# Turning round the second matrix product of a fused attention and MLP kernel: the activations stationary, the weights moving

## The chip, the cores and the metric

The kernel runs on one core of a Trainium2 chip. The metric is the device time of one execution in microseconds (us). The engines are named as the profile names them: PE is TensorE (the matmuls), PEld its loads of the stationary operand, DVE is VectorE, ACT is ScalarE, POOL is GpSimd and SP is SyncE, which issues the DMAs here.

## The reference

An attention with two branches, over q, k and v of 8 batches, 8 heads, 576 positions and 64 channels, feeds a two-layer MLP over 4608 tokens of 512 channels:

```python
q_d = q.reshape(B, H, Sd, factor, D).mean(axis=3)      # factor 4, so do k_d, v_d
out_up = np.repeat(sm_attn(q_d, k_d, v_d), factor, axis=2)
mask = np.abs(pos[:, None] - pos[None, :]) < factor    # a band of 7 keys
scores = np.where(mask, scale * np.matmul(q, k.transpose(0, 1, 3, 2)), -1e9)
attn_out = out_up + softmax(scores) @ v
x = attn_out.transpose(0, 2, 1, 3).reshape(B * S, H * D)
h = x @ w_in                                           # 512 x 2048
g = np.maximum(0.01 * h, h)
return g @ w_out                                       # 2048 x 512
```

## The kernel before

**Precision.** Both products of the MLP are made from operands that are split in a high and a low part in the fp32r format (xh and xl, wih and wil, gh and gl, woh and wol). Each product of two tiles is then three matmuls: high x high, high x low and low x high.

**Tiling.** The 4608 tokens are cut in twelve chunks: chunk 0 of 512 tokens (worked in two halves of 256, `TOP`), chunk 1 of 256 and ten chunks of 384. The 2048 hidden channels are cut in 16 blocks f of 128. `STEPS` lists (chunk, first and last token, f): 48 steps of 256 tokens and 160 of 384. In chunk 0 the first half runs eight blocks ahead of the second, so the first half is through with f = 15 while the second is at f = 7 (`LEAD` is 8).

**The first product** is `up_proj` (matmuls on line 811). For each step it takes a PSUM bank `hp` (two of them) and writes 128 hidden channels x n tokens in it, with w_in stationary and x moving: 4 blocks of input channels x 3 = 12 matmuls. `leaky` follows: two activations on ACT (lines 822 and 823) write gh and the full-precision value back to the bank, and one subtraction on DVE (line 825) writes gl and gives the bank back. gh and gl have three buffers each.

**The second product** is `down_proj` (matmuls on line 847). For each step it takes gh and gl, and for each of four blocks e of 128 output channels makes three matmuls with a 128 x 128 piece of w_out stationary and the n tokens moving. Output channel block e gathers in bank `acc{e}`, over all 16 steps of the chunk: four banks, one buffer each, used again by the next chunk. In chunk 0 both halves of 256 tokens share a bank, so all four are evacuated at the chunk's end. With two banks `hp`, two banks `pt` for the attention and four accumulators, all eight banks of PSUM are in use.

**The output.** `store` copies a bank to SBUF (line 876 on ACT; line 873 on DVE for every second block of the first and the last chunk) and issues one DMA. The buffer is `o`, with two buffers of 384 tokens. Chunk 0's four copies of 512 tokens go to an old token buffer, `x0`, which `outbuf` holds until they have been sent. The output in memory is channels x tokens, and the host transposes it.

**The order of the work.** Every part is a Python generator, and `Order.run` lists the instructions of each engine in an order that it works out from estimated durations (`COST` for ACT, DVE and POOL; for PE the number given at the place; for DMAs a formula in `run`), from ranks, and from when buffers come free. `up_proj` has rank 4999 and `down_proj` 5000, behind all the attention's work. The engines then run these fixed lists, each waiting for its semaphores. A change in one estimate can therefore move instructions anywhere.

**The rest.** Batch 0's attention is made with matmuls, for the other seven the band's products are made on POOL (lines 669 and 730) and summed on DVE (675 and 736). The weights are loaded, converted and split in the first 115 us (lines 287 to 308). `landing` puts finished tokens in x (lines 767 to 782); x has two buffers, `x0` and `x1`.

Of the kernel before, what the change touches and what calls it, by code (L numbers as in the profile page):

```python
# [21 lines left out]
BLK, NBLK = 9, 64  # L22
# [12 lines left out]
LEAD = 8  # L35
HEADS = 2
FREE = 9
LSPLIT = 14
HALFS = 4
HF1 = 21  # L40
# [155 lines left out]
def attn_moe(ctx: ExitStack, tc, qkt, vd, qb, kb, vb, vwb, band, identb, w_in, w_out, ident, edge, out):  # L196
# [4 lines left out]
    ps = ctx.enter_context(tc.tile_pool(name="ps", bufs=1, space=PSUM))  # L201

    bufs = dict(head=HEADS, qk=1, vs=1, qk_d=2, qblk=1, v_d=2, su_vd=2, su_half=1, st_d=2, pd=1, ptd=2, outd=2, q=2, k=2, v=2, s=3, st_l=3, prod=2, up=1,
                xloc=2, lst=3, gh=3, gl=3, o=2, hp=2, pt=2, x0=1, x1=1, stage=3, stage2=4, acc0=1, acc1=1, acc2=1, acc3=1,
                su_vw=NC, su_vs=NC, su_pt=2)
    od = Order(bufs)

    def slot(*tags):
        return (yield ("slot", tags, 0))
# [5 lines left out]
    def bank(s):  # L215
        return ps.tile([128, 512], F32, name=s.tag, tag=s.tag, bufs=bufs[s.tag])
# [572 lines left out]
    def up_proj():  # L789
        i = 0  # L790
        while i < len(STEPS):
            ch, a, z, f = STEPS[i]
            n = z - a
            per = 0.012 + n / 2400
            m = 2 if (ch, a, f) == (0, 0, 0) else 1
            if f == 0:
                tx = 0.0 if m > 1 else (yield from wait(("x", ch, a), LANDED[ch, a]))
            hps = []
            for k in range(m):
                tw = yield from wait(("w", f + k, 0))  # L800
                s_h = yield from slot("hp")
                hps.append((s_h, bank(s_h), weight(f + k, 0), tw))
            xh, xl = (x[:, :, a:z] for x in xt[ch])
            for c in range(NC):
                if m > 1:
                    tx = yield from wait(("x", 0, 0, c))
                ws = slice(c * 128, (c + 1) * 128)
                for k, (s_h, hp, w, tw) in enumerate(hps):
                    t = yield from op("PE", 3 * per, tx, tw, s_h.t)
                    for j, (h, x) in enumerate(((1, xh), (1, xl), (0, xh))):  # L810
                        nc.tensor.matmul(hp[:, :n], w[h][:, ws], x[:, c], start=c + j == 0, stop=c == NC - 1 and j == 2)  # L811
                    if c == NC - 1:
                        od.spawn(-10, leaky(i + k, n, s_h, hp, t))
            if f == NF - 1:
                od.signal(("done", ch), t)
            i += m
# [12 lines left out]

    def down_proj():  # L830
        for i, (ch, a, z, f) in enumerate(STEPS):
            n = z - a
            last = z == CHUNKS[ch][1]
            per = 0.012 + n / 2400
            tg = yield from wait(("g", i))
            tw = yield from wait(("w", f, 1))
            s_g, s_l, gh, gl = gs.pop(i)
            w = weight(f, 1)
            for e in range(NE):
                if (a, f) == (0, 0):  # L840
                    s_a = yield from slot(f"acc{e}")
                    accs[ch, e] = s_a, bank(s_a)
                s_a, acc = accs[ch, e]
                es = slice(e * 128, (e + 1) * 128)
                t = yield from op("PE", 3 * per, tg, tw, s_a.t)
                for j, (h, g) in enumerate(((1, gh), (1, gl), (0, gh))):
                    nc.tensor.matmul(acc[:, a:z], w[h][:, es], g[:, :n], start=(a, f, j) == (0, 0, 0),  # L847
                                     stop=f == NF - 1 and j == 2, skip_group_check=ch == 0)
                if f == NF - 1 and last:
                    od.spawn(-5, store(ch, e, s_a, acc, t))  # L850
            s_g.free(t)
            s_l.free(t)

    first = []

    def outbuf():
        yield from wait(("xbuf", 0))
        s_x = yield from slot("x0")
        first.append(sb(s_x, [128, NE, 512], F32))
        od.signal("first", s_x.t)  # L860
        s_x.free((yield from wait("sent", NE)))

    def store(ch, e, s_a, acc, t):
        base, n = CHUNKS[ch][:2]
        if ch == 0:
            s_o, to = None, (yield from wait("first"))
            o = first[0][:, e]
        else:
            s_o = yield from slot("o")
            o, to = sb(s_o, [128, OMAX], F32)[:, :n], s_o.t  # L870
        if ch in (0, len(CHUNKS) - 1) and e % 2:
            t = yield from op("DVE", n, t, to)
            nc.vector.tensor_copy(out=o, in_=acc[:, :n])  # L873
        else:
            t = yield from op("ACT", n, t, to)
            nc.scalar.copy(out=o, in_=acc[:, :n])
        s_a.free(t)
        t = yield from load(out[e * 128:(e + 1) * 128, base:base + n], o, 512 * n, t)
        if s_o:
            s_o.free(t)  # L880
        else:
            od.signal("sent", t)

    su = tc.tile_pool(name="su", bufs=1)
    sup = su.__enter__()
# [15 lines left out]
    with tc.manual_schedule():  # L901
# [19 lines left out]
        od.spawn(0, edges())  # L921
        od.spawn(0, opened())
        od.spawn(30, over())
        od.spawn(-1, outbuf())
        od.spawn(5000, down_proj())
        od.spawn(4999, up_proj())
        for b in range(BANDED, B):
# [10 lines left out]
    attn_moe.order = od  # L938


_OUTS = [((DM, B * S), 'float32')]
# [58 lines left out]
```

## Time and profile before

| | |
|---|---|
| median of 3 runs | 939.52 us (938.36 to 941.15) |
| the profiled execution | 939.17 us, of which the span from first to last instruction 937.4 us |
| granted TensorE clock, mean | 0.991 |
| PE busy | 911.9 us, 97% |
| DVE, ACT, POOL busy | 598.3, 428.8, 610.4 us |
| data read and written in HBM | 104.47 and 9.44 MB |

The profile shows one execution. A group's row gives the line in the kernel, the engine, the operation, the tiles written and read, the number of instructions, then the busy time and the mean duration in ns, then the idle time of the engine ahead of them and what ended it. Matmuls overlap, so the duration of one is no measure of its price: the distance between starts is. In the list of waits each row has the waiting instruction, what it waited for, the sum in us, the number of times and the longest. In the chain that ended last a row has its start in us, its length and the number of instructions merged in it. In the timeline a row has start and duration in us, and in brackets the idle time ahead of it.

### The profile page before, as it was taken

The numbers are of one execution on the slowest core, as the hardware profiler recorded it, in microseconds if no ns is written. First come the engines' busy times: TensorE is split into PE (matmuls) and PEld (weight loads), VectorE is DVE, ScalarE is ACT, GpSimd is POOL, SyncE is SP. The second block draws the span as 40 slices with busy tenths as digits, with TensorE's granted clock in tenths as the row PEclk, the third lists the DMA queues.
The fourth block names the chain that finished last, engine by engine and source line by source line (L and its number), as shares of the span: only waits on it lengthen the run. The fifth ranks groups of instructions, "written<-read, shape, count | busy, mean of one in ns | idle before, by whom it ended". The sixth has DMA issues, their size and how long they took to land.

```text
span 937.4 us, 16213 instructions
## 1 busy us (share of the span) xinstructions
PE 911.9 (97%) x6114; PEld 892.3 (95%) x6114; DVE 598.3 (64%) x934; ACT 428.8 (46%) x1178; POOL 610.4 (65%) x349
## 2 busy tenths in 40 slices
PE   6898999999999999999999999999999999999997
PEld 4698999998999999999999999999999999999997
DVE  5999998898978876864655873862754744211111
ACT  4876755655546444654324553523423424312221
POOL 4677899999989978963975963983984972000000
PEclk7999999999999999999999999999999999999999
DMA  9886656656554652541432541530431410000000
GB/s 255 265 280 204 197 171 184 183 159 204 150 154 151 205 155 78 184 148 57 138 91 55 182 154 32 152 113 27 131 103 36 141 51 12 34 1 1 35 1 35
DMA packets 58783, 114.97 MB, mean 123 GB/s; under 512 B 6976, under 2 KB 23616, under 8 KB 58704
## 3 DMA queue, kind: packets, MB, share of 16 engines
q1 hardware_dynamic: 58704, 113.93, 40.1%
q8 instruction: 48, 0.79, 0.4%
q14 instruction: 31, 0.25, 0.1%
HBM read 104.47 MB, written 9.44 MB: 122 GB/s over the span
## 4 chain that ended last, share of the span: by engine, by line
PE 89%; DVE 2%; ACT 0%; issue 0%; DMA 0%; DVEq 0%; ACTq 0%
PE hp L811 41%; PE acc L847 41%; PE pt L418 2%; PE pt L455 2%; PE pt L479 2%; PE pt L767 1%; DVE gl L825 0%; DMA out_dram<-o 0%; DVE stage L295 0%; DVE v_d L369 0%; DVE x L295 0%; DVE s L675 0%; DVE x L873 0%; ACT pd L434 0%; DVE qblk L385 0%
## 5 line engine op out<-in xcount | busy, mean ns | idle before, releaser
L811 PE MATMUL hp<-x,wih 128*128 128x384 f32 (+1 forms) x1664 | 406.7, 329 | 7.2 <-DVE gl L825 7.2
L669 POOL TENSOR_TENSOR prod<-q,k 128x1344 f32<-128x1344 f32 x84 | 260.6, 3103 | 84.1 <-DVE xloc L736 68.1
L811 PEld LDWEIGHTS hp<-x,wih 128*128 128x128 f32 x1664 | 287.2, 189 | 10.0 <-DVE gl L825 8.3
L730 POOL TENSOR_TENSOR prod<-v,s 128x1344 f32<-128x1344 f32 x84 | 262.3, 3126 | 20.0 <-DVE xloc L736 19.7
L847 PE MATMUL acc<-gh,woh 128*128 128x384 f32 (+1 forms) x832 | 272.4, 327 | 0.0
L811 PE MATMUL hp<-x,wil 128*128 128x384 f32 (+1 forms) x832 | 269.7, 324 | 0.2 <-POOL wil L308 0.2
L847 PE MATMUL acc<-gh,wol 128*128 128x384 f32 (+1 forms) x832 | 268.8, 323 | 0.0
L847 PE MATMUL acc<-gl,woh 128*128 128x384 f32 (+1 forms) x832 | 268.8, 323 | 0.0
L825 DVE TENSOR_TENSOR gl<-hp,gh 128x384 fp32r<-128x384 f32 (+1 forms) x208 | 108.5, 523 | 248.8 <-ACT hp L823 247.4
L822 ACT ACTIVATE gh<-hp 128x384 fp32r<-128x384 f32 (+1 forms) x208 | 97.4, 468 | 296.3 <-PE acc L847 289.1
L811 PEld LDWEIGHTS hp<-x,wil 128*128 128x128 f32 x832 | 157.1, 189 | 0.6 <-POOL wil L308 0.6
L847 PEld LDWEIGHTS acc<-gh,woh 128*128 128x128 f32 x832 | 156.5, 188 | 0.7 <-issue 0.4
L847 PEld LDWEIGHTS acc<-gl,woh 128*128 128x128 f32 x832 | 156.5, 188 | 0.0
L847 PEld LDWEIGHTS acc<-gh,wol 128*128 128x128 f32 x832 | 156.4, 188 | 0.0
L675 DVE TENSOR_REDUCE s<-prod 128x21 f32<-128x1344 f32 x84 | 129.3, 1539 | 7.0 <-POOL prod L669 6.9
L736 DVE TENSOR_REDUCE xloc<-prod 128x192 f32<-128x1344 f32 x84 | 129.5, 1541 | 5.9 <-POOL prod L730 5.8
L823 ACT ACTIVATE hp<-hp 128x384 f32<-128x384 f32 (+1 forms) x208 | 96.5, 464 | 0.0
L434 ACT ACTIVATE pd<-pt,st_d 128x144 f32<-128x144 f32 x84 | 32.0, 381 | 47.5 <-DVE st_d L431 36.3
L754 ACT COPY up<-outd 128x576 f32<-128x576 f32 x84 | 52.2, 675 | 0.1
L774 DVE TENSOR_TENSOR pt<-pt,up 128x384 f32<-128x384 f32 x42 | 37.8, 899 | 22.3 <-PE pt L767 18.5
L457 ACT COPY ptd<-pt 72x288 f32<-72x288 f32 x64 | 25.0, 397 | 31.6 <-PE pt L455 31.3
L369 DVE TENSOR_REDUCE v_d<-vs 72x128 f32<-72x512 f32 x56 | 37.5, 669 | 1.3 <-DMA vs<-in_vd_dram 1.2
(111 smaller groups left out, 709.4 us busy)
## 6 DMA issues: line engine op xcount, KB each, us to landing
k<-in_kb_dram SPq DMA_DIRECT2D x84, 288.0 KB
v<-in_vb_dram SPq DMA_DIRECT2D x84, 288.0 KB
qk<-in_qkt_dram SPq DMA_DIRECT2D x32, 576.0 KB
vs<-in_vd_dram SPq DMA_DIRECT2D x56, 144.0 KB
q<-in_qb_dram SPq DMA_DIRECT2D x84, 96.0 KB
out_dram<-o SPq DMA_DIRECT2D x40, 192.0 KB
x<-in_w_in_dram SPq DMA_DIRECT2D x10, 511.8 KB
x<-in_w_out_dram SPq DMA_DIRECT2D x7, 511.8 KB
```

Source lines behind the costliest of these rows:

```text
L369: nc.vector.tensor_reduce(out=v_d[:, p0:p1], in_=vs, axis=AX.X, op=ALU.add)
L669: nc.gpsimd.tensor_tensor(out=prv, in0=q[:, a - j0:z - j0].unsqueeze(2).to_broadcast([128, n, W, D]), in1=view(k, (a - j0) * D, [[D, n], [ ...
L675: nc.vector.tensor_reduce(out=s[:, p, a - j0:z - j0], in_=prv, axis=AX.X, op=ALU.add)
L730: nc.gpsimd.tensor_tensor(out=prv, in0=view(v, 0, [[1, nj], [nv, D], [1, W]]), in1=s[:, p, :nj].unsqueeze(2).to_broadcast([128, nj, D, W]) ...
L736: nc.vector.tensor_reduce(out=xl_t[:, :nj, p], in_=prv, axis=AX.X, op=ALU.add)
L754: nc.scalar.copy(out=up[:, pp], in_=outd[b][:, 2 * u + pp].unsqueeze(2).to_broadcast([128, SD, FAC]))
L774: nc.vector.tensor_tensor(out=xv, in0=xv, in1=upv, op=ALU.add)
L811: nc.tensor.matmul(hp[:, :n], w[h][:, ws], x[:, c], start=c + j == 0, stop=c == NC - 1 and j == 2)
L822: nc.scalar.activation(out=gh[:, :n], in_=hp[:, :n], func=AF.Prelu, alpha=0.01)
L823: nc.scalar.activation(out=hp[:, :n], in_=hp[:, :n], func=AF.Prelu, alpha=0.01)
L825: nc.vector.tensor_tensor(out=gl[:, :n], in0=hp[:, :n], in1=gh[:, :n].bitcast(F32), op=ALU.subtract)
L847: nc.tensor.matmul(acc[:, a:z], w[h][:, es], g[:, :n], start=(a, f, j) == (0, 0, 0), stop=f == NF - 1 and j == 2, skip_group_check=ch == 0)
```

## The change

The second product is turned round. A 128-token slice of g is now the stationary operand, and 512 columns of w_out (all output channels) move. A bank holds 128 tokens x 512 channels instead of 128 channels x n tokens. Each step makes 3 matmuls for each tile of 128 tokens (9 for 384 tokens, 6 for 256) where it made 12. The three products are now in the order gh x woh, gh x wol, gl x woh.

A chunk of 384 tokens needs three banks, and takes any of `acc0` to `acc2`, whichever comes free first; chunk 0 takes all four, two for each half. From chunk 1 on the first product may take `acc3` as a bank beside the two `hp`.

The output is stored as tokens x channels. Each bank is copied in two halves of 256 channels, with one DMA each, through `o`, which now has three buffers of 256 columns in the place of two of 384. Both copies are on ACT; in the last chunk the second is on DVE. `outbuf` is gone, so the token buffer `x0` isn't held for chunk 0's output. The planner's estimate for one matmul of 512 columns is 0.226 us.

```diff
+ACC = tuple(f"acc{e}" for e in range(4))
...
-                xloc=2, lst=3, gh=3, gl=3, o=2, hp=2, ...
+                xloc=2, lst=3, gh=3, gl=3, o=3, hp=2, ...
...
-                s_h = yield from slot("hp")
+                s_h = yield from slot("hp", *(ACC[3:] if ch else ()))
...
     def down_proj():
         for i, (ch, a, z, f) in enumerate(STEPS):
...
-            for e in range(NE):
-                if (a, f) == (0, 0):
-                    s_a = yield from slot(f"acc{e}")
-                    accs[ch, e] = s_a, bank(s_a)
-                s_a, acc = accs[ch, e]
-                es = slice(e * 128, (e + 1) * 128)
-                t = yield from op("PE", 3 * per, tg, tw, s_a.t)
-                for j, (h, g) in enumerate(((1, gh), (1, gl), (0, gh))):
-                    nc.tensor.matmul(acc[:, a:z], w[h][:, es], g[:, :n], start=(a, f, j) == (0, 0, 0),
-                                     stop=f == NF - 1 and j == 2, skip_group_check=ch == 0)
-                if f == NF - 1 and last:
-                    od.spawn(-5, store(ch, e, s_a, acc, t))
+            for m in range(a, z, 128):
+                if f == 0:
+                    s_a = yield from slot(*(ACC[:3] if ch else ACC))
+                    accs[ch, m] = s_a, bank(s_a)
+                s_a, acc = accs[ch, m]
+                t = yield from op("PE", 3 * 0.226, tg, tw, s_a.t)
+                for j, (h, g) in enumerate(((1, gh), (0, gh), (1, gl))):
+                    nc.tensor.matmul(acc, g[:, m - a:m - a + 128], w[h], start=f + j == 0, stop=f == NF - 1 and j == 2)
+                if f == NF - 1:
+                    od.spawn(-5, store(ch, m, s_a, acc, t))
...
+    def store(ch, m, s_a, acc, t):
+        row = CHUNKS[ch][0] + m
+        for h in range(2):
+            es = slice(h * DM // 2, (h + 1) * DM // 2)
             s_o = yield from slot("o")
+            o = sb(s_o, [128, DM // 2], F32)
+            if ch == len(CHUNKS) - 1 and h:
+                t = yield from op("DVE", DM // 2, t, s_o.t)
+                nc.vector.tensor_copy(out=o, in_=acc[:, es])
+            else:
+                t = yield from op("ACT", DM // 2, t, s_o.t)
+                nc.scalar.copy(out=o, in_=acc[:, es])
+            if h:
+                s_a.free(t)
+            s_o.free((yield from load(out[row:row + 128, es], o, 131e3, t)))
...
-        od.spawn(-1, outbuf())
```

More of the change, by code (lines that the diff above doesn't have):

```diff
@@ L203, in attn_moe @@
     bufs = dict(head=HEADS, qk=1, vs=1, qk_d=2, qblk=1, v_d=2, su_vd=2, su_half=1, st_d=2, pd=1, ptd=2, outd=2, q=2, k=2, v=2, s=3, st_l=3, prod=2, up=1,
-                xloc=2, lst=3, gh=3, gl=3, o=2, hp=2, pt=2, x0=1, x1=1, stage=3, stage2=4, acc0=1, acc1=1, acc2=1, acc3=1,
+                xloc=2, lst=3, gh=3, gl=3, o=3, hp=2, pt=2, x0=1, x1=1, stage=3, stage2=4, acc0=1, acc1=1, acc2=1, acc3=1,
                 su_vw=NC, su_vs=NC, su_pt=2)
@@ L831, in down_proj @@
         for i, (ch, a, z, f) in enumerate(STEPS):
-            n = z - a
-            last = z == CHUNKS[ch][1]
-            per = 0.012 + n / 2400
             tg = yield from wait(("g", i))
@@ L851, in down_proj @@
             s_g.free(t)
             s_l.free(t)
[L854 to L868, printed above, removed]
-            s_o = yield from slot("o")
[L870 to L882, printed above, removed]
+    def store(ch, m, s_a, acc, t):
+        row = CHUNKS[ch][0] + m
+        for h in range(2):
+            es = slice(h * DM // 2, (h + 1) * DM // 2)
+            s_o = yield from slot("o")
+            o = sb(s_o, [128, DM // 2], F32)
[8 more added lines that the diff above has]
+            s_o.free((yield from load(out[row:row + 128, es], o, 131e3, t)))
@@ L938, in attn_moe @@
     attn_moe.order = od
-_OUTS = [((DM, B * S), 'float32')]
+_OUTS = [((B * S, DM), 'float32')]
 def kernel(q, k, v, moe_w_in, moe_w_out):
@@ L995 @@
     r = _run(nc, [arrays], core_ids=[0])
-    o = r.results[0]["out_0_dram"].reshape(DM, B, S)
-    head = o[:, :BANDED].reshape(DM, BANDED * S).T
-    rest = o[:, BANDED:].reshape(DM, B - BANDED, BLK, NBLK).transpose(1, 3, 2, 0).reshape((B - BANDED) * S, DM)
-    return np.concatenate([head, rest], axis=0)
+    o = r.results[0]["out_0_dram"]
+    rest = o[BANDED * S:].reshape(B - BANDED, BLK, NBLK, DM).transpose(0, 2, 1, 3).reshape((B - BANDED) * S, DM)
+    return np.concatenate([o[:BANDED * S], rest], axis=0)
```

## The prediction

> **What bounds the kernel now.** I read the page first, engines and slices, then the chain that ended last, then the waits of PE alone, and last the places in time where those waits lie.
>
> ```profile
> PE 911.9 (97%) x6114; PEld 892.3 (95%) x6114; DVE 598.3 (64%) x934; ACT 428.8 (46%) x1178; POOL 610.4 (65%) x349
> ...
> PE   6898999999999999999999999999999999999997
> ...
> PEclk7999999999999999999999999999999999999999
> ...
> PE 89%; DVE 2%; ACT 0%; issue 0%; DMA 0%; DVEq 0%; ACTq 0%
> PE hp L811 41%; PE acc L847 41%; PE pt L418 2%; PE pt L455 2%; PE pt L479 2%; PE pt L767 1%; DVE gl L825 0%; DMA out_dram<-o 0%; DVE stage L295 0%; DVE v_d L369 0%; DVE x L295 0%; DVE s L675 0%; DVE x L873 0%; ACT pd L434 0%; DVE qblk L385 0%
> ```
>
> TensorE is the bound: busy in 97% of the span, 89% of the chain, and the two GEMMs (L811 and L847) are 41% of the chain each. The granted clock is full in nearly every slice. "Busy" doesn't say that every matmul runs at its best, so the price of one must be read from the distance between them. The 25.5 us in which PE is idle (937.4 - 911.9) are in its waits and at the two ends:
>
> ```profile
> PE hp L811 <- DVE gl L825: 7.2, 5, 2.6
> PE hp L534 <- DMA band_sb<-in_band_dram: 5.1, 1, 5.1
> PE pt L455 <- ACT ptd L457: 1.8, 2, 1.4
> PE pt L455 <- POOL v L442: 1.6, 1, 1.6
> PE pt L534 <- DVE xloc L550: 1.1, 1, 1.1
> PE pt L569 <- POOL xloc L561: 0.7, 2, 0.4
> PE pt L455 <- ACT outd L485: 0.7, 2, 0.5
> PE acc L584 <- ACT su_pt L571: 0.5, 1, 0.5
> PE hp L811 <- POOL wil L308: 0.2, 1, 0.2
> ```
>
> These nine rows are all of it, 18.9 us. None waits for the attention's tokens (x), and none for an evacuated accumulator bank (acc from L873 or L876). So TensorE's own time can shrink without the supply showing at once. The one group that the change can touch is the first: the first GEMM waits for a bank hp, which the residual (L825) gives back. Three of its five waits are the large ones:
>
> ```profile
> 80.55 0.50 PE L811 MATMUL hp<-x,wih 128*128 128x256 f32 x2 [2.63 <-DVE gl L825]
> ...
> 161.27 1.40 DVE L873 COPY x<-acc 128x512 f32<-128x512 f32 x2 [0.97 <-PE acc L847]
> ...
> 162.86 0.73 DVE L825 TENSOR_TENSOR gl<-hp,gh 128x256 fp32r<-128x256 f32 x2
> ...
> 163.31 0.50 PE L811 MATMUL hp<-x,wih 128*128 128x256 f32 x2 [1.38 <-DVE gl L825]
> ...
> 220.60 0.28 PE L847 MATMUL acc<-gh,wol 128*128 128x256 f32 x1
> ...
> 221.02 0.38 ACT L434 ACTIVATE pd<-pt,st_d 128x144 f32<-128x144 f32 x1
> ...
> 221.35 0.52 ACT L822 ACTIVATE gh<-hp 128x384 fp32r<-128x384 f32 x1
> ...
> 222.89 0.62 PE L811 MATMUL hp<-x,wih 128*128 128x384 f32 x2 [2.01 <-DVE gl L825]
> ```
>
> At 163 the residual stood on DVE behind two copies of chunk 0's output, 1.40 us together. From 220.9 (220.60 + 0.28) to 222.9 both hp banks were full: their activation (L822) stood on ACT behind the attention's exponentials (L434). The wait that ends at 80.55 is in chunk 0.
>
> **The change, the matmuls.** Counts by shape and distances between matmuls:
>
> ```profile
> L847 PE MATMUL acc<-gh,woh 128*128 128x384 f32 x640 | 217.4, 340 | 0.0
> ...
> L847 PE MATMUL acc<-gh,woh 128*128 128x256 f32 x192 | 54.9, 286 | 0.0
> ```
>
> ```profile
> 87.29 3.18 PE acc L847 x27
> ...
> 416.95 4.16 PE hp L811 x24
> 421.11 4.16 PE acc L847 x24
> ```
>
> The second GEMM has three such groups, so 3 x 640 = 1920 matmuls of 384 columns and 3 x 192 = 576 of 256, together 2496. After it there are 36 token tiles x 16 blocks of w_out x 3 products = 1728 of 512 columns: 768 fewer, with the same number of columns in all. The durations 340 and 286 ns overlap and are no price. The chain gives it: 4.16/24 = 173.3 ns for 384 columns, 3.18/27 = 117.8 for 256. The line through both is 6.8 ns for a matmul and 0.4336 ns for a column, so 512 columns take 228.8 ns, an estimate, since no row has that shape.
> - A step of 384 tokens: 12 x 173.3 = 2079.6 before, 9 x 228.8 = 2059.2 after: 20.4 ns less, 160 times: 3.3 us.
> - A step of 256 tokens: 12 x 117.8 = 1413.6 before, 6 x 228.8 = 1372.8 after: 40.8 ns less, 48 times: 2.0 us.
>
> Sum 5.2 us (which is 768 x 6.8 ns), and PE is on the path nearly everywhere. One bound: cost in proportion to columns from the 384 row (0.4513 ns), so 231.1 ns for 512; the 384 steps then save nothing, the 256 steps 27 ns, 1.3 us in all. The other bound is the best rate by column that any stretch shows. Twelve matmuls of 256 columns in a row, of which these are the first and the last, start 1.24 us apart from end to end:
>
> ```profile
> 45.65 0.28 PE L847 MATMUL acc<-gh,woh 128*128 128x256 f32 x1
> ...
> 46.89 0.28 PE L847 MATMUL acc<-gh,wol 128*128 128x256 f32 x1
> ```
>
> 1.24/11 = 112.7 ns, 0.4403 ns for a column, so 225.4 ns for 512; then the 384 steps save 51 ns and the 256 steps 61 ns, 11.1 us in all. I take the line: it uses both shapes as they run nearly all the time, and falls between the bounds.
>
> On TensorE: Matmul & The Clock Gate, section Back-to-back issue gap, the Trainium skill gives a stream N/2.4 + 2.5 ns at the full clock. That is 109.2 ns for 256 columns and 162.5 for 384, where the trace has 117.8 and 173.3, so it doesn't agree here. By the page only 2.5 ns hang on the number of matmuls, and the saving would be 768 x 2.5 = 1.9 us.
>
> Each matmul loads its stationary operand (6114 loads to 6114 matmuls), and turning the product round makes g that operand. A load shows 188 ns, and matmuls of 256 columns run 117.8 ns apart with it, so loads overlap further than one matmul; 228.8 ns leave more cover. I cost it at nothing. Were a load bare once per step it would be up to 0.19 us x 208 = 39 us, but the residual is done a step or more ahead of its use, and the waits of PE hold no row of L847.
>
> ```profile
> L847 PEld LDWEIGHTS acc<-gl,woh 128*128 128x128 f32 x832 | 156.5, 188 | 0.0
> ```
>
> **The change, banks and copies.** Chunk 0's first 256 tokens now have banks of their own and leave eight steps earlier, and no copy of chunk 0 goes to DVE. So the two copies ahead of the residual at 161 are gone: 1.4 us, between 0 and 1.4. From chunk 1 on the fourth accumulator bank is a third hp bank, so at 220.9 a further step of the first GEMM (12 x 173.3 ns = 2.1 us) can go ahead while ACT is late: 2.0 us, between 0 and 2.0. Next late there is g itself, with three buffers as before. The wait at 80.6 lies in chunk 0, where hp stays at two banks; I leave it.
>
> The copies out of the accumulators and their transfers:
>
> ```profile
> L876 ACT COPY o<-acc x42: 372/481/498, 222.9 to 932.0; 128x384 f32<-128x384 f32 x38, 128x256 f32<-128x256 f32 x4
> ...
> L876 ACT COPY x<-acc x2: 607/608/609, 162.9 to 163.4; 128x512 f32<-128x512 f32 x2
> ```
>
> ```profile
> L231 SPq DMA_DIRECT2D out_dram<-o x44: 332/343/433, 223.4 to 933.2; - x44
> ```
>
> The 48 copies before (44 on ACT, and 4 on DVE, two of them shown above and two below) become 72 of 256 columns, 3 of them on DVE; the transfers likewise. ACT: 38 x 0.48 + 4 x 0.37 + 2 x 0.61 = 20.9 us before, 69 x 0.37 = 25.5 after, 4.6 us more on an engine that is busy 46%: hidden. SP issues 24 more transfers at 0.34 us, 8.2 us over the whole span, behind which loads of q, k and v queue; these run ahead, since PE never waits for x. Three output buffers for six pieces of a chunk mean that the 4th to 6th copy of a chunk wait for a landing, and what stands behind them on ACT is the activation of the first GEMM (L822). That wait exists already with two buffers:
>
> ```profile
> 928.86 0.34 PE L847 MATMUL acc<-gh,woh 128*128 128x384 f32 x1
> ...
> 929.58 0.48 ACT L876 COPY o<-acc 128x384 f32<-128x384 f32 x1 [3.74 <-PE acc L847]
> ...
> 930.08 3.50 SPq L231 DMA_DIRECT2D out_dram<-o  x4
> 930.10 0.56 DVE L873 COPY o<-acc 128x384 f32<-128x384 f32 x1 [3.67 <-PE acc L847]
> ...
> 932.05 0.48 ACT L876 COPY o<-acc 128x384 f32<-128x384 f32 x1 [2.00 <-DMA out_dram<-o]
> 932.66 0.56 DVE L873 COPY o<-acc 128x384 f32<-128x384 f32 x1 [2.01 <-DMA out_dram<-o]
> ```
>
> **The tail.** Let S be the start of the last step, 928.86 before; its last copy ended at 932.66 + 0.56 = S + 4.36. A buffer is free 1.99 us after its copy ended (930.06 to 932.05). After the change the three products of a tile take 0.69 us and the last shows its result about 0.40 us after its start, so the tiles are ready at S + 0.86, 1.55 and 2.24. A copy takes 0.37 us on ACT; on DVE about 0.42, worked out from 0.70 for 512 columns and 0.56 for 384. If the DVE copy of a tile follows the ACT copy, they end at 1.23 and 1.65, 1.92, 3.64 (waits for the first buffer), then 4.01 and 4.43. That is 0.1 us later than before, 0 if the two run side by side. What follows the last copy, 4.2 us, stays.
>
> **The sum.** Against the profiled execution's 939.17 us (span 937.4, 1.8 around it; the median of the runs is 939.52, so nothing is to be corrected): -5.2 matmuls, -1.4 and -2.0 waits, +0.1 tail, and +0.4 for about one new short wait at a chunk's end: -8.1, so 931 us. The program that orders the work replans everything from changed costs, which can shift single waits of the first 150 us (the 2.63 us above is such a one) either way; that is +-3 us.
>
> **The rivals.**
> 1. Cost in proportion to columns: the matmuls give 1.3 us and not 5.2, so 935 us. For it: only two shapes are measured, and 384 columns already cost 0.4513 ns each against 0.4602 for 256, a small difference. Against: both lie on many equal distances. The Trainium skill's gap rule (the page and section above) would land near it, at 934.4.
> 2. Three accumulator banks for three tiles make a turn-round wait, and the kernel gets slower. The fourth bank no longer covers the end of a chunk. With both copies on ACT the first bank is free at S + 1.6, but the second tile's second copy waits for the first landing: 1.23 + 1.99, then 0.37, so 3.6. If the next chunk's first down step follows at once (S + 2.06), its second tile would start at 2.75 and waits 0.85 us. Nine boundaries join chunks of three tiles: 7.7 us, which eats the gain to 939. Each further 1 us until a landing, for instance behind loads of k and v, adds 9 us; from about 2.4 us per landing the result is slower, and at 2.8 us it is 946. Against: the planner's own formula in run() charges such a transfer 1.2 + 131/265 + 0.8 = 2.5 us, more than the 1.99 measured, and so it puts a step of the first GEMM (2.1 us) between when one is at hand; a third hp bank makes that likelier.
> 3. More than forecast: 225.4 ns for 512 columns (11.1 us) give 925 us, and if the replanning takes the wait of 2.63 us away too, 922.5. For it: the stretch at 45 us. Against: it is short, and the long stretches later on are 5 ns slower.
> 4. The plan of the first 150 us gets worse by as much as the waits give: about 937, no change.
>
> **How the numbers follow.** Forecast 0.55 (928 to 934), rival 1 0.13, rival 2 0.10 (two thirds of it slower), rival 3 0.12, rival 4 0.10 (half no change, the rest split). A measurement of this kernel tells about 0.3%, 2.8 us, from no change, so faster means below 936.7: 0.55 + 0.13 + 0.12 and a little of rival 4, 0.81. Slower 0.08, no change 0.11. The range from 924.5 to 938.5 takes in rival 1, most of rivals 3 and 4, and leaves out rival 2.
>
> **What would show it.** Right: 1728 matmuls of the second GEMM whose chain pieces are near 228.8 ns apart (36 in 8.24 us); no copy on DVE before the last chunk; in the waits of PE the row of hp at about 4 us or less; no row of acc waiting for ACT; last copy about 4.4 us after the last step's start. Wrong: distances of 231 ns or more (rival 1) or below 227 (rival 3); rows "PE acc from ACT o" with some ten counts and more than 4 us (rival 2); the first step of chunk 2 starting later than before relative to 222.9 (rival 4).

## The result: slower by 0.7%

The changed kernel takes 946.23 us (median of 4 runs, 943.86 to 946.53) against 938.94 us of the kernel before on the same chip: a ratio of 1.0071, 95% interval 1.0043 to 1.0099. The forecast was 931.0 us, with a range of 924.5 to 938.5 and a chance of 0.08 for slower. The profiled execution took 946.23 us, its span is 944.3 us, 6.9 more than before (937.4).

The profile after, the lines that answer to those shown of before. First the page's engines, clock and chain:

```profile
PE 918.2 (97%) x5346; PEld 816.9 (87%) x5346; DVE 601.1 (64%) x933; ACT 431.2 (46%) x1203; POOL 610.0 (65%) x349
...
PEclk7998999999999999999999999999999999999999
...
PE 89%; DMA 3%; DVE 2%; issue 2%; POOL 1%; ACT 1%; SPq 0%; DVEq 0%; POOLq 0%; ACTq 0%
```

There are 768 fewer matmuls, as the change says, and yet PE is busy for 6.3 us more. So it is the price of what is left that has to be read. The chain gives it, at a place where steps follow each other with nothing between:

```profile
418.19 4.20 PE acc L844 x18
422.39 4.18 PE hp L812 x24
```

4.20/18 = 233.3 ns for a matmul of 512 columns, where 228.8 was forecast and 231.1 was the upper bound; 4.18/24 = 174.2 for 384. Then the waits of PE:

```profile
PE hp L535 <- DMA band_sb<-in_band_dram: 5.4, 1, 5.4
PE hp L812 <- issue: 3.6, 1, 3.6
PE hp L812 <- DVE gl L826: 2.6, 1, 2.6
PE pt L456 <- POOL v L443: 1.7, 1, 1.7
PE pt L456 <- ACT outd L486: 1.6, 2, 1.1
PE acc L844 <- ACT o L861: 1.6, 2, 1.3
...
PE hp L812 <- POOL wil L309: 0.4, 1, 0.4
```

The waits at 161 and 220 us are gone, as forecast: the two large rows of hp that are left lie in chunk 0, at 82 and 109 us. They weigh nearly what the five of before did: 3.6 + 2.6 against 7.2. The one at 82 has "issue" as its releaser, so the profile shows no event for it; the one at 109 ends with the subtraction (L826). Each is followed by a stretch at a lower clock:

```profile
78.44 3.59 issue
82.03 5.46 PE hp L812 x24
...
108.91 4.48 PE hp L812 x24
```

Twenty-four matmuls of 256 columns take 5.46 and 4.48 us here, where 24 x 117.8 = 2.83 is the price at full clock: the wait of 3.6 us costs another 2.6, that of 2.6 another 1.6. The kernel before has one such stretch, behind its wait that ends at 80.55. The same stretches of before and after, granted clock in the column ahead of the DMA share:

```profile
78.00:90.00 12.00, 9.45 (x67) 9.45 (x68) 11.58 (x14) 6.50 (x15) 9.92 (x6) 0.86 0.63 178
...
100.00:116.00 16.00, 16.00 (x142) 15.68 (x141) 14.61 (x25) 12.20 (x35) 12.47 (x9) 1.00 0.54 175
```

```profile
78.00:90.00 12.00, 8.39 (x44) 7.72 (x43) 8.48 (x11) 6.06 (x17) 7.75 (x5) 0.72 0.78 270
...
100.00:116.00 16.00, 13.37 (x84) 12.10 (x82) 12.78 (x18) 8.75 (x26) 11.63 (x6) 0.89 0.41 122
```

The Trainium skill (TensorE: Matmul & The Clock Gate, section Part 1: The HAM clock gate) says that TensorE's clock is halved after an idle window of about 3.4 us and comes back after a busy one. The half-clock stretches ahead of the last matmul are 3.4 us long or a multiple of it (10.2 and 3.4 us in the trace of before; 10.2, 3.4, 6.8 and 3.4 in that of after), which agrees; here a wait of 2.6 us was enough for one of 3.4.

Last, the turn-round wait of rival 2, seen in the timeline at the end of a chunk:

```profile
606.50 0.38 ACT L861 COPY o<-acc 128x256 f32<-128x256 f32 x1 [1.34 <-PE acc L844]
...
607.21 0.37 ACT L861 COPY o<-acc 128x256 f32<-128x256 f32 x1 [0.33 <-PE acc L844]
...
608.47 0.65 ACT L861 COPY o<-acc 128x256 f32<-128x256 f32 x2
...
609.17 0.50 PE L844 MATMUL acc<-woh,gh 128*128 128x512 f32 x1 [1.30 <-ACT o L861]
...
610.25 0.38 ACT L861 COPY o<-acc 128x256 f32<-128x256 f32 x1 [1.14 <-DMA out_dram<-o]
```

The first chunk's banks leave through three buffers; the next chunk's first tile wants a bank, and its matmul stands 1.30 us until ACT has made a copy. There are nine boundaries between chunks of three tiles, but it happens at two (532 us, there the second tile, and 609 us), 1.6 us in all.

**Where the 6.9 us are.** By the starts of the first product's steps in the two traces: the first step of the MLP starts 2.7 us later (36.9 against 34.2), the next 64 steps take the same (250.0 against 250.2), steps 64 to 200 take 5.0 us more (609.9 against 604.9), the end 0.6 less. The first of these is scatter between executions: the run with the order of products undone, below, started at 34.5. The 5.0 us are steady: the runs below with the same order of instructions and g misaligned take 610.0 and 610.4. Of them 1.6 are the turn-round waits. But they are not the price of the matmuls alone. A step's start also moves with the attention's work that the plan puts ahead of it: the kernel with chunk 0 alone turned, below, takes 609.8 us here, and its matmuls in these steps are the old ones.

A second count is less open to this: the time from each matmul's start to the start of the next one on PE, less the waits, and the waits by themselves.

| us | before | after |
|---|---|---|
| second product, with the tail | 411.9 | 414.6 |
| first product | 413.3 | 415.5 |
| attention's matmuls | 93.2 | 93.7 |
| PE's waits | 19.0 | 20.5 |

Nearly all of the first product's 2.2 us lies ahead of chunk 2 (76.0 against 74.0 us), where the half-clock stretches are.

### The profile page after: what moved, and what is told of

The parts are those of the page before. It is cut to its first block, busy times and chain, and to the rows that moved or that the text cites. A ratio compares the mean times of both kernels' runs of the same rounds, so it can differ in the third digit from the quotient of the medians.

```text
span 944.3 us, 14788 instructions
## 1 busy us (share of the span) xinstructions
PE 918.2 (97%) x5346; PEld 816.9 (87%) x5346; DVE 601.1 (64%) x933; ACT 431.2 (46%) x1203; POOL 610.0 (65%) x349
## 4 chain that ended last, share of the span: by engine, by line
PE 89%; DMA 3%; DVE 2%; issue 2%; POOL 1%; ACT 1%; SPq 0%; DVEq 0%; POOLq 0%; ACTq 0%
PE acc L844 41%; PE hp L812 29%; PE acc L812 12%; PE pt L419 2%; PE pt L456 2%; PE pt L480 2%; PE pt L768 1%; DMA su_vs<-in_vd_dram 1%; DMA x<-in_w_in_dram 1%; DMA prod<-in_w_in_dram 1%; POOL wil L309 1%; DVE stage L296 0%; DVE x L296 0%; POOL wol L309 0%; SPq L232 0%
## 5 line engine op out<-in xcount | busy, mean ns | idle before, releaser
L812 PE MATMUL hp<-x,wih 128*128 128x384 f32 (+1 forms) x1208 | 291.9, 327 | 6.2 <-issue 3.6
L844 PE MATMUL acc<-woh,gh 128*128 128x512 f32 x576 | 232.3, 403 | 1.6 <-ACT o L861 1.6
L844 PE MATMUL acc<-woh,gl 128*128 128x512 f32 x576 | 227.6, 395 | 0.0
L844 PE MATMUL acc<-wol,gh 128*128 128x512 f32 x576 | 227.6, 395 | 0.0
L812 PEld LDWEIGHTS hp<-x,wih 128*128 128x128 f32 x1208 | 211.3, 191 | 14.9 <-issue 4.8
L826 DVE TENSOR_TENSOR gl<-hp,gh 128x384 fp32r<-128x384 f32 (+1 forms) x151 | 77.2, 514 | 148.5 <-ACT hp L824 142.6
L844 PEld LDWEIGHTS acc<-woh,gl 128*128 128x128 f32 x576 | 108.1, 188 | 25.6
L844 PEld LDWEIGHTS acc<-woh,gh 128*128 128x128 f32 x576 | 108.4, 188 | 21.4 <-ACT o L861 2.5
L844 PEld LDWEIGHTS acc<-wol,gh 128*128 128x128 f32 x576 | 108.5, 188 | 18.3
L812 PE MATMUL acc<-x,wih 128*128 128x384 f32 (+1 forms) x456 | 116.4, 338 | 0.0
L812 PEld LDWEIGHTS acc<-x,wih 128*128 128x128 f32 x456 | 80.6, 188 | 3.1 <-DVE x L783 0.2
L826 DVE TENSOR_TENSOR gl<-acc,gh 128x384 fp32r<-128x384 f32 (+1 forms) x57 | 31.0, 544 | 73.9 <-ACT acc L824 67.9
```

Of the source, the lines that this page charges most:

```text
L826: nc.vector.tensor_tensor(out=gl[:, :n], in0=hp[:, :n], in1=gh[:, :n].bitcast(F32), op=ALU.subtract)
L844: nc.tensor.matmul(acc, g[:, m - a:m - a + 128], w[h], start=f + j == 0, stop=f == NF - 1 and j == 2)
```

## The experiments

Times are medians, ratios are against the kernel before on the same chip with their 95% interval. Kernels named "matmuls alone" leave the rest of the kernel out. The theory at the start was that the matmuls of 512 columns are dearer than forecast; the rivals were that the replanned chunk 0 or the turn-round waits make the loss.

**What a matmul of each width costs by itself.** 96 matmuls in a row for each width, fp32r, stationary and moving operand changing each time:

```diff
+    for i in range(N):  # n512
+        nc.tensor.matmul(A(i), G(i), w[:, i % 8], **S(i))
```

> Leaves the whole computation out: only rows of 96 matmuls in fp32r with random operands, nothing else running, one row per width (256, 384, 512, 320, 448, 128, 480 columns) and, for 512 columns, rows with one stationary tile, one moving tile, zeros moving, 24 in a row on one bank, two halves of 256, and bf16. Theory 1 (the price is a matter of the width alone): start to start 118 ns at 256, 173 at 384, 233 at 512, the same whatever is stationary and whichever bank is written; two halves of 256 cost 236 for both. Rival A (the turned operands, their neighbours or three in a row on one bank make it dear): 512 columns cost 227 to 229 in the plain row, and one of the variant rows 233. Rival B (a current limit that depends on the data): zeros moving run at 227 or less, random data at 233.

```profile
39.22 16.64 PE acc L44 x96
55.86 21.80 PE acc L46 x96
...
257.99 20.74 PE acc L68 x96
278.72 15.60 PE acc L70 x96
```

These rows are 384 and 512 columns in fp32r, then 512 and 384 in bf16. The distances between starts, once steady: 120.0 ns for 256 columns, 146.7 for 320, 173.3 for 384, 202.7 for 448, 226.7 for 512. One stationary operand, one moving operand, zeros or one bank changed nothing. So alone 512 columns are cheaper than the forecast's 228.8, and the 233.3 of the kernel is something of the kernel's. In bf16 it was 215.8 and 162.5: the rule of the Trainium skill that the prediction names (TensorE: Matmul & The Clock Gate, section Back-to-back issue gap, N/2.4 + 2.5 ns) holds for bf16 to the tenth, and fp32r costs 10.8 ns more. (The section calls it the gap of an isolated matmul; here it holds for rows of 96.)

**The third hp bank undone.**

```diff
-                s_h = yield from slot("hp", *(ACC[3:] if ch else ()))
+                s_h = yield from slot("hp")
```

> The changed kernel without the third bank for the first product. Theory 1 (the loss lies in the plan of the first 120 us, where the third bank isn't in use, and in the dearer matmul): chunk 0 runs as in the changed kernel, and the wait of about 2 us near 220 us is back: 947 to 948.5 us. Rival (the third bank reorders PE's work and does the harm): 940 to 943 us.

946.98 us, ratio 1.0067 (1.0045 to 1.0088): the bank is worth nothing that can be measured, and doesn't hurt. The wait near 220 us was expected back and didn't come: no wait of the first product after 110 us is longer than 0.3 us in this run either.

**Each half of the change alone.** Chunk 0 in the old way and the others turned, then chunk 0 turned and the others in the old way, with two hp banks and copies in halves:

```diff
+            if ch == 0:
+                for e in range(NE):
...
+            else:
+                for m in range(a, z, 128):
```

> Chunk 0's second product as before (w_out stationary, four banks, copies of 512 columns), all other chunks turned round. Every engine's order is that of the kernel before up to the end of chunk 0. Theory 1: no new waits before 150 us; from chunk 2 on 160 steps cost 2.10 and not 2.08 us, so 3.2 us more, the wait at 220 us (2.0) goes, the tail is 0.8 shorter: 939 to 941 us. Rival 2 (the turned product loses all along, at the chunk ends or in its loads): 944 us or more.

> Chunk 0's second product turned round, all other chunks as before (their copies in two halves of 192 columns through the three buffers). Every engine's order is that of the changed kernel up to the end of chunk 0. Theory 1: the waits of chunk 0 and the halved clock behind them are there, about 5 us more, the wait at 161 us (1.4) may go, the rest is as before: 942 to 944.5 us. Rival 2: 937 to 940 us.

945.03 us (1.005, 1.003 to 1.007) and 945.24 us (1.0042, 1.0026 to 1.0057). The first expectation missed: with chunk 0 as before the loss stays, at what rival 2 gave. Steps 64 to 200 take 609.8 us, as in the changed kernel, but they do so in the second kernel too, with the old matmuls, so this number doesn't tell the price of the matmuls from the plan. The second came out just above its range; the waits of 3.6 and 2.6 us in chunk 0 are there in it, and not in the first, whose longest is 2.5. Half a change each costs most of the whole, so the two do not add; the replanned order costs something in either. PE's waits for an accumulator, first and second kernel:

```profile
PE acc L861 <- ACT o L908: 1.7, 2, 1.3
```

```profile
PE acc L849 <- ACT o L893: 2.1, 2, 1.9
```

The second has old matmuls with four banks from chunk 1 on, and still the turn-round wait: it comes with the copies in halves through three buffers, whichever way the matmuls are turned.

**Width changing from step to step.** Matmuls alone again, steps of 384 and of 512 columns in turn:

> Leaves the whole computation out: rows of fp32r matmuls alone on the chip, 14 steps each. The first such run had 512 columns settle at 226.7 ns after some ten matmuls at 224 to 236 ns that followed a row of another width. Theory W (a change of width unsettles the spacing, and runs of 9 to 18 between steps of 384 columns never settle): the row of 512 alone in the changed kernel's order of operands runs at 227 ns, the rows of 12 x 384 then 9 x 512 and 24 x 384 then 18 x 512 at 231 to 234, 12 x 512 then 9 x 512 at 227, and 12 x 384 then 12 x 384 at 173.3. Rival S (the same g loaded twice in a row, or the triple of operands, makes it dear): the row alone already has 231 to 234, and the rows with both products of high w first have 227. Rival K (it needs the kernel around it: semaphores, other engines, transfers): every row of 512 has 227.

```profile
99.86 2.08 PE acc L60 x9
101.94 2.10 PE hp L57 x12
```

The nine of 512 take 231.2 ns each and the twelve of 384 take 175.5; eighteen and twenty-four in turn take 228.9 and 174.4; 512 after 512 takes 226.7. After a change of width the distances run between 224 and 236 ns for some ten matmuls and then settle. That looked like the cause (theory W in the later expectations), but 2 ns were missing.

**The order of the three products put back.**

```diff
-                for j, (h, g) in enumerate(((1, gh), (0, gh), (1, gl))):
+                for j, (h, g) in enumerate(((1, gh), (1, gl), (0, gh))):
```

> The changed kernel with the three products in the order of before, high w twice, then low w; nothing else, and the plan is the same instruction by instruction. Theory W: no difference, 945 to 947 us, 512 columns at 233 ns. Rival S: 512 columns at 227 ns, 6.5 ns x 1728 = 11 us less, 934 to 936 us.

945.22 us, 1.0051 (1.0035 to 1.0066), and the row of eighteen still takes 4.20 us. The order isn't it.

**Conversions in two parts**, meant to shorten what stands ahead of the subtraction in chunk 0, in the changed kernel and in the kernel before:

```diff
-        t = yield from op("DVE", 780, t)
...
+        for p in (slice(0, DM // 2), slice(DM // 2, DM)):
+            t = yield from op("DVE", 390, t)
```

> The changed kernel with each conversion on VectorE (the shift and or on 512 columns) cut in two of 256, so that the residual can go between and a stretched conversion is half as long. If the waits of chunk 0 come from conversions of 2 to 3.5 us standing ahead of the residual: the waits of PE on hp before 120 us fall from 6.2 us to 2 to 4, the halved clock after them falls with it, and the time to 942 to 944.5 us. If they come from something else (the plan's order alone): 945 to 948 us.

> The kernel before with the same cut. Its one wait of this kind is 2.6 us with 3.4 us of halved clock behind it: if the cut helps, 937.5 to 940 us; if the replanning only shuffles waits, within 1.5 us of before on either side.

961.53 us (1.0229, 1.0203 to 1.0255) and 947.78 us (1.0081, 1.0056 to 1.0107): both slower, and outside every range that was given. DVE's groups in the first 200 us, whole in the changed kernel and split:

```profile
L296 DVE SCALAR_TENSOR_TENSOR x<-x,head 128x512 int32<-128x512 int32 x17 | 20.1, 1198 | 3.9 <-ACT head L294 3.6 <-issue 0.3
```

```profile
L297 DVE SCALAR_TENSOR_TENSOR x<-x,head 128x256 int32<-128x256 int32 x34 | 28.9, 871 | 1.8 <-ACT head L294 1.3 <-issue 0.2
```

Half an instruction takes 0.87 us where the whole took 1.20, so DVE has 8.8 us more of them on this tile alone, and PE is busy 38.6 of the 50 us from 50 to 100 where it was 46.0. So chunk 0 seems to hang on DVE's conversions; what makes the waits of 3.6 and 2.6 us was not found.

**Steps in pairs; estimates changed.** In chunks 2 to 11 two steps of the first product and then two of the second, as one piece each for the planner. Beside it, one number of the planner changed in the kernel after and in the kernel before:

```diff
+                t = yield from op("PE", 18 * 0.229, *ts)
+                for k, (fk, (s_g, s_l, gh, gl), w) in enumerate(use):
+                    for m in range(a, z, 128):
...
-                t = yield from op("PE", 3 * 0.226, tg, tw, s_a.t)
+                t = yield from op("PE", 3 * 0.2333, tg, tw, s_a.t)
...
-            per = 0.012 + n / 2400
+            per = 0.0133 + n / 2400
```

> The kernel after, with the steps of chunks 2 to 11 taken two at a time: 24 matmuls of the first product (two steps) and then 18 of the second, so the matmul width changes half as often; same matmuls, same banks. Theory W (each change between 384 and 512 columns unsettles the spacing): 512 columns fall from 233.3 to 229 to 231 ns and 384 stays at 174.4 or less. Per pair of steps 18 x 2.3 to 18 x 4.4 ns, 41 to 79 ns, times 80 pairs: 3.3 to 6.3 us off 946, so 940 to 943 us. A theory that 512 columns simply cost 233.3 ns in this kernel (its neighbours on other engines, not the order): spacing unchanged and 945 to 947 us. If the coarser steps make new waits of TensorE (for a g or an hp bank), these add to either figure and stand in the list of waits; the spacing then decides.

> The kernel after with one number of the planner changed: 0.2333 us for a matmul of 512 columns, as measured, in the place of 0.226. Theory P (much of the loss is the luck of the replanned first 150 us, which the estimates decide): the waits of chunk 0 move and the time with them, 942 to 945 us, or as far the other way. Theory W: the price of the matmuls is what it is, 945 to 948 us, and 512 columns stay at 233 ns. Both allow a shift of 2 to 3 us by single waits; below 942 would speak for P.

> The kernel before with the planner's constant for a matmul 0.0133 us in the place of 0.012, so 173.3 ns for 384 columns, as measured; nothing else. It shows what a replanning alone does to the kernel before. Theory P: any replanning costs the kernel before 2 to 4 us, since its waits happen to fall well: 941 to 944 us. Theory W: the loss of the change is in its matmuls, and the kernel before stays within 2 us of itself: 938 to 942 us.

943.26 us (1.0026, 1.001 to 1.0042), 947.48 (1.008, 1.0059 to 1.0102) and 942.45 (1.0027, 1.0011 to 1.0043). The pairs came within their range, but not for its reason:

```profile
425.55 4.20 PE acc L858 x18
```

Still 233.3 ns, with eighteen in a row, and the 18th to the 35th of longer rows no better. Theory W alone falls: alone they would have settled. The turn-round wait of 1.6 us is gone from the pairs; where the rest of their gain comes from was not taken apart. The better estimate gained nothing in the changed kernel, and the kernel before lost 2.6 us by one alone, so a few us of any such change are the planner's.

**What is different in the kernel.** Matmuls alone, one thing of the kernel at a time:

> Matmuls alone, the rest of the kernel left out, so only the distances between starts count. The run with the steps in pairs kept 512 columns at 233 ns even 18 to 36 in a row, and so do the last 90 us of the kernel after, where DVE, ACT and POOL are nearly idle; alone they settled at 226.7. What is different in the kernel is looked for one at a time, 72 matmuls of 512 columns each: moving and stationary operand at the places in SBUF that the kernel has (w_out at 56448, g at 154048; w at 180032), the kernel's PSUM banks 2, 3 and 6, both together, operands that hold the low parts of a split, and activations and subtraction beside. Theory N (a neighbour in memory or the place of the operands decides): one of these rows goes to 231 to 236 ns, and it names the cause. Theory W (the width changes alone): all of them settle at 226.7, and only the last but one row, 12 of 384 and 9 of 512 in turn with high and low parts mixed as in the kernel, is above, near 231.

```profile
35.96 16.36 PE bk L55 x72
52.32 16.80 PE bk L57 x72
69.12 16.73 PE bk L59 x72
85.85 16.80 PE bk L61 x72
102.65 16.35 PE bk L63 x72
```

In order: low places, the kernel's places for w and g, w at 180032 with the kernel's g, w low with the kernel's g, the kernel's banks. 16.80/72 = 233.3 ns, the kernel's own number, with the pattern 231, 236, 231, 236 that the kernel has; 16.35/72 = 227.1, with the unsettled start in it. Every row with g at 154048 is dear, whatever the moving operand; banks, low parts and the activations beside do nothing.

**Is it the place?** Eight places for the stationary operand alone, then g moved in the kernel, in the kernel before as a control, and in the pairs, the order of all instructions kept:

```diff
-    wk = ctx.enter_context(tc.tile_pool(name="wk", bufs=1))
+    gpool, wk = (ctx.enter_context(tc.tile_pool(name=n, bufs=1)) for n in ("gpool", "wk"))
...
-        gh, gl = sb(s_g, [128, OMAX], F32R), sb(s_l, [128, OMAX], F32R)
+        gh, gl = sb(s_g, [128, OMAX], F32R, gpool), sb(s_l, [128, OMAX], F32R, gpool)
```

> Matmuls alone, the rest of the kernel left out: 60 matmuls in a row for each row, 512 columns with the stationary operand at eight places (43008, 65536, 98304, 120832, 131072, 141312, 154048 and 190464 bytes into a partition), then the moving operand high (172032, 202752), then 448, 384 and 256 columns with the stationary operand high, then 384 columns moving from high places. Theory N2 (a stationary operand that lies above some place makes 512 columns dear): 226.7 ns at the low places and 232 to 234 from one place on, between 120832 and 154048; 384 columns stay at 173.3 either way, since the kernel before shows 173.3 with g at 154048. Theory D (the distance between the two operands decides): with the moving operand at 172032 and g at 190464, both high and near each other, 226.7 again.

> The kernel after with gh and gl in a pool of their own ahead of the working buffers, at 81088 to 90304 in the place of 154048 to 163264; the order of the instructions on every engine is the same, instruction by instruction. Theory N2 with W (place and change of width both count): 512 columns fall from 233.3 to between 228 and 231.2 ns, as alone between steps of 384, so 1728 x 2.1 to 5.3 ns, 3.6 to 9.2 us off 946: 937 to 942.5 us. N2 alone: 226.7 ns, 11.5 us less, 934.5 us. If place has nothing to do with it in the kernel: 233 ns and 945 to 947 us.

> The control: the same move of gh and gl in the kernel before, with the same order of the instructions. There g moves, with 384 columns at 173.3 ns, and no row alone showed less than that for 384 columns. Theory N2: no change, 938 to 941 us. If low places help in some other way than through the stationary operand of 512 columns (transfers, the other engines), the kernel before gains too, and the gain of the run with g low is no proof.

> Steps in pairs and g at the low places together. Alone, 24 of 384 and 18 of 512 in turn gave 174.4 and 228.8 ns. Theory N2 with W: 512 columns at 228 to 229 ns, 1728 x 4.5 to 5.3 ns, 7.8 to 9.2 us off the 943.3 of the pairs: 934 to 935.5 us, which would be faster than the kernel before. If the place doesn't count: 943 us.

```profile
97.95 13.60 PE bk L63 x60
111.55 13.73 PE bk L65 x60
125.29 13.60 PE bk L67 x60
```

These are 141312, 154048 and 190464: 226.7, 228.9 and 226.7 ns. So a high place is not dear, only 154048 is. In the kernels 512 columns stayed at 232 to 233 ns: 943.16 us (1.0039, 1.0022 to 1.0056), which lies between the ranges, so the price has to decide; control 939.69 (0.9998, 0.9982 to 1.0015), pairs 944.15 (1.0045, 1.0028 to 1.0062). The theory of a high place falls. What is left is what 154048 and the new place, 81088, share: both are 64 bytes past a multiple of 128. The seven cheap places are multiples of 128. (The control left g 64 bytes off as well, so it says nothing of alignment.)

**Alignment.** gh and gl in a pool ahead of all others, at 384 to 9600, each buffer at a multiple of 128 bytes; the first without, the second with the steps in pairs:

```diff
-    const = ctx.enter_context(tc.tile_pool(name="const", bufs=1))
+    gpool, const = (ctx.enter_context(tc.tile_pool(name=n, bufs=1)) for n in ("gpool", "const"))
```

> The kernel after with gh and gl in a pool ahead of all others, at 384 to 9600 bytes, each buffer at a whole multiple of 128 bytes; the order of the instructions on every engine is the same, instruction by instruction. The w_out blocks f 0 to 8 lie at multiples of 128 too, blocks 9 to 15 are 32 bytes short of one, as before. Theory A (a stationary operand 64 bytes off a multiple of 128 makes 512 columns dear) with W (a change of width unsettles the distance for some ten matmuls, which alone gave 231.2 ns for 9 between steps of 384): in steps f 0 to 8 512 columns fall from 233 to between 226.7 and 231.2 ns, and long rows of them settle at 226.7; in steps 9 to 15 the same or less of it. Then 972 x 2 to 1728 x 6.6 ns, 2 to 11 us off 945: 934 to 943 us. If alignment doesn't count in the kernel: 232 to 233 ns everywhere and 943 to 947 us.

> The same alignment of g with the steps in pairs, which took 943.3 us with 233.2 ns for 512 columns. Theory A with W: 228.8 ns, as alone with 24 of 384 and 18 of 512 in turn, or 226.7 where rows are longer: 972 x 4.5 to 1728 x 6.6 ns, 4.4 to 11.4 us less, 932 to 939 us, so at or below the kernel before. If alignment doesn't count: 943 us.

941.78 us (1.0004, 0.9985 to 1.0023) and 939.33 us (0.9983, 0.9966 to 0.9999), the second just above its range. The chain of the first at the place shown for the changed kernel, blocks f 6 and 7 of w_out, then 8 and 9; and of the pairs, 36 in a row:

```profile
413.14 4.09 PE acc L844 x18
417.24 4.17 PE hp L812 x24
421.41 4.16 PE acc L844 x18
```

```profile
678.60 8.17 PE acc L858 x36
```

4.09/18 = 227.2 and 8.17/36 = 226.9 ns. By blocks of w_out, from chunk 2 on: blocks 0 to 8, which are aligned as well, take 227.1 to 229.3 ns in the first kernel, where the changed kernel has 232.4 to 233.3; blocks 9 to 15, which lie 32 bytes short of a multiple of 128, take 233.4 to 234.7, where it has 231.1 to 233.4. Steps 64 to 200 take 606.7 us in the place of 609.9, with the same order of instructions, and by the second count the second product of chunks 2 to 11 takes 342.0 us in the place of 345.3; the kernel before has 342.1. So g's alignment is the cause of the dear matmuls in the blocks 0 to 8.

In the blocks 9 to 15 aligning g gains nothing. That w_out's own place is the reason there is argued and not shown, since no run has these blocks aligned. For it speaks a row of the run with eight places. There 384 columns were taken with g at 154048 stationary, then moving as in the kernel before, then with both operands at multiples of 128:

```profile
193.29 10.40 PE bk L77 x60
203.69 10.59 PE bk L79 x60
214.28 10.42 PE bk L81 x60
```

The moving operand that is 64 bytes off takes 176.5 ns, where the other two take 173.3 once steady. Against it, 384 columns moved from 154048 in the kernel before too, and took 173.3 there.

The first kernel is level with the kernel before, and the pairs with g aligned are ahead of it by 0.2%, which is less than the 0.3% that a measurement tells. The kernel before with g aligned was not run.

Not tried: blocks 9 to 15 aligned too. An estimate from the rows above, if they then cost what blocks 0 to 8 do: 7/16 of 1728 matmuls, 756, by 5 to 6 ns, about 4 us.

## Why the prediction was wrong, point by point

**The matmuls (-5.2 us): the step that failed.** "I take the line: it uses both shapes as they run nearly all the time, and falls between the bounds." The line gave 228.8 ns, the kernel has 233.3, outside both bounds. A step of 384 tokens costs 9 x 233.3 = 2100 ns against 2080, a step of 256 tokens 6 x 233.3 = 1400 against 1414: 160 x 20 - 48 x 14 = +2.5 us in the place of -5.2. The line itself was not far wrong: alone, aligned and in long rows the shape takes 226.7, and the saving would be 160 x 39 + 48 x 53 = 8.9 us, more than forecast. (With the 120.0 ns that 256 columns take when aligned, the same line gives 226.6.) But even aligned, nine between twelves of 384 take 231.2 alone, at which a step of 384 tokens saves nothing; the working had no price for the change of width. What the prediction didn't see is that turning the product made g the stationary operand, in buffers 64 bytes off, and that an operand's place can cost up to 6.6 ns of each matmul (233.3 against 226.7). No row of before could show it. But the bounds were drawn from two shapes in the old roles only, and the roles were changed: that should have widened the upper one. Rival 1 (231.1 ns) had the direction, not the cause.

**The two waits (-1.4 and -2.0): gone, one of them by luck, and given back.** That the third bank took away the wait at 220 us is not shown: with two hp banks it is gone as well, and with three and chunk 0 in the old way a wait of 1.3 us ends at 222.5. It fell to the new plan. For the wait at 161 either part of the change was enough: with chunk 0 in the old way the two copies still stand ahead of the residual on DVE, 1.40 us, and PE doesn't wait, since it goes on in the third bank; with two banks the copies are gone. But the sum of PE's waits for hp fell only from 7.2 to 6.2 us. The prediction left chunk 0's wait as it was and gave +-3 us for the plan; the wait of 2.6 us at 80.6 became one of 3.6, a new one of 2.6 came at 109, and each brought a half-clock stretch on top of itself, which was not in the working. This is what rival 4 spoke of.

**The turn-round wait (+0.4): 1.6 us.** Rival 2's mechanism is there, at two of nine boundaries. At six of the other seven the planner puts one step of the first product or more between, as the prediction said of it.

**The tail (+0.1): -0.8, in another place than the working looked.** From the start of the last matmul of the second product to the end of the span it is 5.8 us, before 6.6. The last copy ends 4.9 us after the last step's start, 0.5 later than forecast; what follows it was to stay at 4.2 us and takes 2.8.

**ACT's 24 more copies and SP's 24 more transfers at nothing: right.** ACT is 46% busy as before, and no wait of PE names them but the turn-round.

**The sum.** By the second count: the second product +2.7 us, of which +2.5 matmuls, -0.8 tail and 1.0 that was not taken apart (the attention's matmuls interrupt its rows more often, 46 times from chunk 2 on where it was 28; chunk 0 turned alone, with the old matmuls and 46 interruptions too, takes 344.7 us there, the kernel before 342.1); the first product +2.2, nearly all of it where the half clock is; the attention's matmuls +0.5; PE's waits +1.6, of which -1.0 hp, +1.6 turn-round and the rest mostly the attention's. Together that is the 6.9 us, but for rounding. The forecast had -5.1 for the second product with its tail, -3.0 for the waits and nothing for the rest, so of the 15 us between forecast and result 7.8 lie in the second product, 4.6 in the waits and 2.7 in what had no term.

**Left open.** Why 64 bytes cost what they cost: with w at 4096 in the place of 22912, in another run, the same g cost 228.9 and not 233.3, so the place of the other operand has a say. Why a change of width unsettles the distances. What makes the waits of chunk 0. And how much of the 6.9 us is scatter: three kernels with the same order of instructions and the same price of the matmuls (as changed, products in the old order, g at another misaligned place) have medians of 946.2, 945.2 and 943.2, against 938.9, 940.1 and 940.2 of the kernel before beside them.

## What to carry to other kernels

When an operand changes its role, moving to stationary or back, its price in the old role is no bound for the new one: measure the new shape alone, with the operands at the places and with the alignment that the kernel will give them. If a measurement alone and the kernel differ by a few ns per matmul, put the kernel's places, banks and neighbours into the small one, one at a time; here that led to the cause when the runs of the whole kernel had not. And a plan that is worked out anew from a changed number moved the time of the kernel before by 2.6 us, and one and the same plan came out 3 us apart in three builds, so a gain of that size has to be shown in the price of the instructions, not only in the time.

## What was not expected of the hardware

- A stationary operand that begins 64 bytes past a multiple of 128 makes a matmul of 512 fp32r columns take 228.9 to 233.3 ns in the place of 226.7. Where the moving one began 32 bytes short of one, with g aligned, the kernel had 233.4 to 234.7; that this is the reason is not shown by a row of its own.
- It isn't dearer at every width: with g at 154048, 448 columns took 200.0 ns and 256 took 117.8, where the aligned operands of the first run took 202.7 and 120.0 (w was at another place there). The 117.8 ns of the kernel before, one end of the forecast's line, came with g 64 bytes off as well.
- A change of width between 384 and 512 columns unsettles the distances for about ten matmuls: 231.2 ns for nine of 512 between twelves of 384, 226.7 in long rows.
- fp32r costs 10.8 ns more than bf16 at 384 and 512 columns (173.3 and 226.7 against 162.5 and 215.8).
